# First loads of a fused attention and two-layer kernel: queues, order and warm-up

## The chip, the core and the metric

One NeuronCore of a Trainium2 chip runs the whole kernel. The engines named below are TensorE (PE, with its weight loads PEld), VectorE (DVE), ScalarE (ACT) and SyncE (SP). SP only starts DMAs here; ACT computes and can start DMAs too. An engine works through its own instructions in the order in which they are written, so a DMA that waits on ACT's queue holds back what ACT has to compute behind it. The metric is the device time of one execution in microseconds (us), lower is better.

## What is computed

Retention attention without a softmax, over 4 batches, 8 heads, 576 positions and head dimension 64, and then two feed-forward layers over the 2304 tokens, all in float32:

```python
scores = scale * np.matmul(q, k.transpose(0, 1, 3, 2))
Dmat = np.where(rel >= 0, gamma[:, None, None] ** rel[None, :, :], 0.0)
x = np.matmul(scores * Dmat[None], v)          # -> 2304 x 512
h = x @ w_in;  x = (np.maximum(h, 0) + np.log1p(np.exp(-np.abs(h)))) @ w_out
r = np.maximum(x @ w2_in, 0);  out = (r * r) @ w2_out
```

The first layer goes 512 to 2048 to 512, the second likewise.

## The kernel before

The sequences are cut into chunks of 64 positions, and two chunks together are one loaded "chunk c" of 128 tokens, 18 in all. The decay factors are worked into k, v and a table, so attention is a chain over chunks: scores, a mask, a running state and the output.

The first four chunks (`last = 4`) make the first tile of 512 tokens and are written out by hand at the head of the kernel, under `tc.manual_schedule()`, so each engine runs its instructions in exactly the written order. This head is the place of the change. For each chunk c of 0 to 3:

- `early_qk(c)` (L968) loads q and k with head dimension on the partitions, heads 0 to 3 to partitions 0 to 63 (LO) and heads 4 to 7 to 64 to 127 (HI): two DMAs of 256 KB, in rows of 1024 bytes. `early_kv(c)` (L977) loads k and v with tokens on the partitions: one DMA of 512 KB over 128 partitions. Both issue from the sync queue.
- `early_scores(c)` (L992, PE) multiplies k and q of the chunk, `early_mask(c)` (L1013, DVE) applies the causal mask, `early_v(c)` (L1001, DVE) scales v, `early_states(c)` (L1024, PE, kept by ACT at L1030) updates the state, `early_carried(c)` and `early_o(c)` (L1040, L1048, PE) make the output, and `early_x(c)` (L1062, DVE, then a rounding copy on ACT, L1067) multiplies it with a table of factors.
- That table is made in the kernel: `rows_in` holds two rows of factors, `spread_rows()` (L1121) spreads them over partitions by matmuls, ACT copies them out (L1125, L1126), and `scalar_xw` (L1131, ACT) and `make_xw` (L949, DVE) multiply them up. `make_xw(1, 1)` stands on DVE between `early_v(0)` and `early_mask(1)`; `early_x(0)` needs it.

Ahead of the first scores, `keep_warm(n)` runs n dummy matmuls of 512 columns on PE (each counts twice in the trace, as float32 goes through PE in two passes). `cst` holds the mask, the factors of v and two rounding constants (two DMAs of 34.5 KB); the first weights `wi_raw` follow the chunks on the sync queue. Splitting a weight into two reduced-precision parts takes ACT L152, L153, then DVE L157, L160, then ACT L188 and DVE L189. The first real layer matmuls are L1096 (`early_g1`) and the steady loop is L515 and L549.

The framework gives DMAs their completion semaphores in rotation, eight of them shared by both queues: a DMA waits, on the engine that issues it, until the DMA that held its semaphore before has landed. No line of the kernel writes these waits.

Of the kernel before, what the change touches and what calls it, by code (L numbers as in the profile page):

```python
# [16 lines left out]
P = 128  # L17
D = 64
CN = 64
# [21 lines left out]
C_ONE, C_UP, C_VW, C_MASK, C_XW = 0, 1, 2, 74, 138  # L41
# [4 lines left out]
def kernel(  # L46
# [26 lines left out]
    nc = tc.nc  # L73
# [33 lines left out]
    cst = const.tile([P, C_ALL], F32, name="cst")  # L107
# [172 lines left out]
    def pump_load(upto):  # L280
        while n_load[0] < min(upto, len(loads)):
            load_w(*loads[n_load[0]])
            n_load[0] += 1
# [68 lines left out]
    LO, HI = slice(0, P // 2), slice(P // 2, P)  # L352
# [5 lines left out]
    def load_chunk(c):  # L358
        if c < NPR:
            new_chunk(c)  # L360
            for i, src in ((0, qk_t), (2, kv)):
                nc.sync.dma_start(
                    out=chunk[c][:, i:i + 2],
                    in_=src[2 * c:2 * c + 2].rearrange("s p i h c -> (s p) i h c"),
                )
# [563 lines left out]
    def keep_warm(count, n=512):  # L929

        for _ in range(count):
            nc.tensor.matmul(
                cold[:, :n], lhsT=warm[:, :P], rhs=warm[:, :n], start=True, stop=True
            )
# [11 lines left out]
    def make_xw(m, n):  # L946


        nc.vector.scalar_tensor_tensor(  # L949
            out=later[:, m - 1:m - 1 + n],  # L950
            in0=cst[:, x_first].rearrange("p (a b) -> p a b", a=KD).unsqueeze(1)
            .to_broadcast([P, n, KD, CN]),
            scalar=1.0,
            in1=times[:, m - 1:m - 1 + n].unsqueeze(3).to_broadcast([P, n, KD, CN]),
            op0=ALU.mult, op1=ALU.mult,
        )
# [4 lines left out]
    qks, kvs, mixed, kept_s, pbs, pos, xs_of, kept_of = {}, {}, {}, {}, {}, {}, {}, []  # L961
    causal = first_pool.tile([P, P], F32, tag="causal", name="causal", bufs=1)

    def early_tiles(c):
        qks[c] = first_pool.tile([P, 2, 2, HH, CN], F32, tag=f"qk{c}", name="qk", bufs=1)
        kvs[c] = first_pool.tile([P, 2, H, CN], F32, tag=f"kv{c}", name="kv", bufs=1)

    def early_qk(c):  # L968
        for g, half in enumerate((LO, HI)):
            nc.sync.dma_start(  # L970
                out=qks[c][half].rearrange("p i s h c -> p i s (h c)"),
                in_=qk_t[2 * c:2 * c + 2].rearrange("s p i h c -> p i s (h c)")[
                    ..., g * HH * CN:(g + 1) * HH * CN
                ],
            )

    def early_kv(c):  # L977
        nc.sync.dma_start(
            out=kvs[c], in_=kv[2 * c:2 * c + 2].rearrange("s p i h c -> (s p) i h c")
        )  # L980

    def early_scores(c):
        if c % 2:
            pb = pbs[c] = [ps_h.tile([P, 512], F32, tag=f"h{g}", name="pb") for g in range(2)]
        else:
            pb = ps_head.tile([P, 2, 512], F32, tag="pb", name="pb", bufs=1)
            pbs[c] = [pb]
            pb = [pb[:, g] for g in range(2)]
        for hh in range(HH):
            for s, to in enumerate((LO, HI)):  # L990
                for g, rows in enumerate((LO, HI)):
                    nc.tensor.matmul(  # L992
                        pb[g][to, hh * P:(hh + 1) * P],
                        lhsT=qks[c][rows, 1, s, hh, :], rhs=qks[c][rows, 0, :, hh, :],
                        start=True, stop=True, skip_group_check=True,
                    )

    def early_v(c):
        t = kvs[c][:, 1]
        w = vw[:, 2 * c * H:(2 * c + 1) * H]  # L1000
        nc.vector.tensor_tensor(  # L1001
            out=t, in0=t, in1=w.unsqueeze(2).to_broadcast([P, H, D]), op=ALU.mult
        )

    def early_mask(c):
        mixed[c] = first_pool.tile([P, H, P], F32, tag="mixed", name="mixed")
        for g, pb in enumerate(pbs[c]):
            n = H // len(pbs[c])
            if len(pbs[c]) == 1:
                pb = pb.rearrange("p g (h n) -> p (g h) n", n=P)  # L1010
            else:
                pb = pb.rearrange("p (h n) -> p h n", n=P)
            nc.vector.tensor_tensor(  # L1013
                out=mixed[c][:, g * n:(g + 1) * n], in0=pb,
                in1=causal.unsqueeze(1).to_broadcast([P, n, P]), op=ALU.mult,
            )
# [53 lines left out]
    def early_keep(c):  # L1070
        nc.sync.dma_start(out=x0d[:, :, c * P:(c + 1) * P], in_=kept_of[c])
# [40 lines left out]
    def spread_rows():  # L1112
        rows = ps_head.tile([P, 2, 512], F32, tag="po", name="rows", bufs=1)
        to = [
            rows[:, 0, at:at + n * b].rearrange("p (a b) -> p a b", a=n)
            for at, n, b in ((0, KD, CN), (256, SCN - 1, KD))
        ]
        for half in (LO, HI):
            one = slice(half.start, half.start + 1)
            for r, of in zip(to, (row[0][:, 0], row[0][:, 1:, :, 0])):  # L1120
                nc.tensor.matmul(  # L1121
                    r[half], lhsT=ones[one], rhs=of[one],
                    start=r is to[0], stop=True, skip_group_check=True,
                )
        nc.scalar.copy(cst[:, x_first].rearrange("p (a b) -> p a b", a=KD), to[0])  # L1125
        nc.scalar.mul(times, to[1], float(D) ** 0.5)  # L1126

    def scalar_xw(m, n):
        for m in range(m, m + n):
            for a in range(KD):  # L1130
                nc.scalar.activation(  # L1131
                    out=later[:, m - 1, a], in_=cst[:, C_XW + a * CN:C_XW + (a + 1) * CN],
                    func=AF.Copy, scale=times[:, m - 1, a:a + 1],
                )

    with tc.manual_schedule():
        rows_in = xs.tile([P, SCN * KD * CN], F32, tag="xr", name="rows_in")
        for c in range(last):
            early_tiles(c)
        early_qk(0)  # L1140
        for half in (LO, HI):
            nc.scalar.dma_start(out=cst[half, :C_XW], in_=consts[CN:P, :C_XW])
        early_kv(0)
        early_qk(1)
        early_kv(1)
        for r in (0, CN):
            nc.scalar.dma_start(out=rows_in[r:r + 1], in_=consts[r:r + 1, C_XW:])
        nc.scalar.preload_act_table_set("softplus")
        for c in range(2, last):
            early_qk(c)  # L1150
            early_kv(c)
        pump_load(3)
        load_chunk(last)
        nc.vector.memset(causal[LO, CN:], 1.0)
        nc.vector.memset(causal[HI, :CN], 0.0)

        for half, to, of, n in ((LO, 0, 0, SCN), (HI, 0, 1, SCN - 1), (HI, SCN - 1, 0, 1)):
            nc.vector.tensor_copy(
                vw[half, to * H:(to + n) * H], cst[half, C_VW + of * H:C_VW + (of + n) * H]
            )  # L1160
        for s, half in enumerate((LO, HI)):
            nc.vector.tensor_copy(
                causal[half, s * CN:(s + 1) * CN], cst[half, C_MASK:C_MASK + CN]
            )
        keep_warm(6)
        early_scores(0)
        row.append(rows_in.rearrange("p (m a b) -> p m a b", a=KD, b=CN))
        spread_rows()
        keep_warm(1)
        scalar_xw(4, 2)  # L1170
        early_mask(0)
        early_v(0)
        make_xw(1, 1)
        early_scores(1)
        early_states(0)
        early_mask(1)
        early_v(1)
        early_carried(0)
        early_o(0)
        early_x(0)  # L1180
        early_scores(2)
        early_states(1)
        scalar_xw(6, 1)
        early_carried(1)
        early_o(1)
        make_xw(2, 2)
        early_mask(2)
        early_v(2)
        early_x(1)
        scalar_xw(7, 2)  # L1190
        early_scores(3)
        early_states(2)
        early_carried(2)
        early_o(2)
        early_low(0)
        early_mask(3)
        early_v(3)
        begin_words()
        early_keep(0)
        early_x(2)  # L1200
        next(begun[0])
        early_low(1)
        early_keep(1)
        early_states(3)
        early_carried(3)
        early_o(3)
        next(begun[0])
        begun.clear()
        begin_words()
        early_g1(0)  # L1210
        early_x(3)
        next_state(3, 1)
        begin_words()
        early_low(2)
        early_low(3)
        early_keep(2)
        for made in begun:
            next(made)
        early_keep(3)
# [231 lines left out]
```

## Time and profile before

| | us |
|---|---|
| three timed runs | 825.25, 827.16, 827.66 |
| their median | 827.16 |
| profiled execution, its time | 823.74 |
| profiled execution, span of the trace | 822.0 |
| PE busy in the span | 810.8 (99%) |
| DVE busy in the span | 607.2 (74%) |
| ACT busy in the span | 378.9 (46%) |

The profiled execution is a single one, 3.4 us below the median of the timed runs. Busy shares cover stages with different limits; the change touches only the first 20 us or so, so what matters there is read from the chain of waits, the timeline and the stretches of that part. In a timeline row the first number is the start in us, the second the length, and a bracket at the end says how long the engine idled before and what released it.

### The profile page before, as it was taken

To read this page: it belongs to the slowest core of one execution; us is meant where nothing else is said; L and a number is where in the kernel's file an instruction comes from. 1 tells how busy PE (TensorE), PEld (TensorE's weight loads), DVE (VectorE), ACT (ScalarE), POOL (GpSimd) and SP (SyncE) were. 2 spreads that over 40 slices of the span, in tenths; PEclk is the share of its full clock that TensorE was granted. 3 is DMA by queue.
4 is the path that set the end of the run, shared out by engine and by line. 5 is a ranking of instruction groups with operands and counts; after the bars stand their busy time and mean duration, and the time that the engine had idled before them with its cause. 6 is when DMAs were issued, how large, how long until landed. Compare 5 with 4: busy or idle time off the path is not lost.

```text
span 822.0 us, 16243 instructions
## 1 busy us (share of the span) xinstructions
PE 810.8 (99%) x5957; PEld 721.6 (88%) x5957; DVE 607.2 (74%) x1160; ACT 378.9 (46%) x739; POOL 0.2 (0%) x4
## 2 busy tenths in 40 slices
PE   8898999999999999999999999999999999999998
PEld 5777999988888888888999999988999988999887
DVE  4998766646565664646796498998798997787876
ACT  3787666535344543545665221454211554111553
POOL 0000000000000000000000000000000000000000
PEclk9999999999999999999999999999999999999999
DMA  9967554466666655656979387898978889888885
GB/s 238 310 219 239 180 180 124 134 207 215 209 229 213 194 172 188 197 181 211 300 251 300 94 251 248 271 297 285 299 249 254 250 271 282 282 249 249 251 274 170
DMA packets 122802, 189.37 MB, mean 230 GB/s; under 512 B 10466, under 2 KB 68450, under 8 KB 122722
## 3 DMA queue, kind: packets, MB, share of 16 engines
q1 hardware_dynamic: 122560, 188.26, 72.1%
q8 instruction: 47, 0.77, 0.4%
q14 instruction: 31, 0.25, 0.1%
q10 hardware_dynamic: 164, 0.09, 0.1%
HBM read 147.41 MB, written 40.89 MB: 229 GB/s over the span
## 4 chain that ended last, share of the span: by engine, by line
PE 95%; DMA 3%; DVE 1%; ACT 0%; SPq 0%; issue 0%; DVEq 0%; ACTq 0%
PE acc L549 24%; PE ph L515 24%; PE py L685 9%; PE py L758 9%; PE px L685 6%; PE pz L758 6%; PE px L758 6%; PE pz L685 6%; PE po L439 2%; DMA qk<-in_qk_t_dram 1%; PE pb L391 1%; PE st L416 1%; DMA kv<-in_kv_dram 1%; DMA ring<-in_qk_t_dram 1%; SPq L970 0%
## 5 line engine op out<-in xcount | busy, mean ns | idle before, releaser
L515 PE MATMUL ph<-xh,wi 128*128 128x512 f32 (+1 forms) x632 | 144.4, 370 | 1.3 <-DVE wi L189 0.8
L515 PEld LDWEIGHTS ph<-xh,wi 128*128 128x128 f32 x632 | 115.9, 189 | 17.0 <-DVE wi L189 1.2
L549 PE MATMUL acc<-gh,woh 128*128 128x512 f32 (+1 forms) x320 | 120.5, 377 | 0.0
L549 PE MATMUL acc<-gh,wol 128*128 128x512 f32 (+1 forms) x320 | 117.8, 368 | 0.0
L549 PE MATMUL acc<-gl,woh 128*128 128x512 f32 (+1 forms) x320 | 117.8, 368 | 0.0
L534 DVE TENSOR_TENSOR gl<-e,gh 128x512 fp32r<-128x512 f32 (+1 forms) x80 | 51.0, 637 | 71.1 <-ACT gh L533 70.3
L526 ACT ACTIVATE e<-ph 128x512 f32<-128x512 f32 (+1 forms) x80 | 44.3, 554 | 126.4 <-PE ph L515 126.2
L685 PE MATMUL py<-t,sring 128*128 128x384 f32 x432 | 88.3, 338 | 0.0
L515 PE MATMUL ph<-xl,wi 128*128 128x512 f32 (+1 forms) x316 | 78.2, 369 | 0.0
L685 PEld LDWEIGHTS py<-t,sring 128*128 128x128 f32 x432 | 74.8, 188 | 2.5 <-DVE uring L889 0.5
L549 PEld LDWEIGHTS acc<-gh,woh 128*128 128x128 f32 x320 | 60.0, 188 | 8.6
L549 PEld LDWEIGHTS acc<-gh,wol 128*128 128x128 f32 x320 | 60.1, 188 | 7.7
L549 PEld LDWEIGHTS acc<-gl,woh 128*128 128x128 f32 x320 | 60.1, 188 | 6.9
L515 PEld LDWEIGHTS ph<-xl,wi 128*128 128x128 f32 x316 | 58.5, 190 | 7.6
L738 ACT CAST gh<-g 128x384 fp32r<-128x384 f32 x84 | 43.2, 515 | 46.2 <-PE px L758 16.1
L738 ACT CAST gring<-g 128x384 fp32r<-128x384 f32 x84 | 43.2, 515 | 39.9 <-PE py L758 16.2
L685 PE MATMUL pz<-t,sring 128*128 128x384 f32 x288 | 58.3, 334 | 0.0
L685 PE MATMUL px<-t,sring 128*128 128x384 f32 x288 | 58.0, 335 | 0.0
L401 DVE TENSOR_TENSOR ring<-pb,cst 64x256 f32<-64x256 f32 x56 | 23.6, 422 | 44.1 <-PE pb L391 27.2
L706 DVE TENSOR_TENSOR g<-g 128x384 f32<-128x384 f32 x96 | 52.6, 554 | 1.5
L706 DVE TENSOR_TENSOR gring<-g,gring 128x384 fp32r<-128x384 f32 x84 | 46.2, 553 | 9.5 <-ACT gring L738 8.3
L706 DVE TENSOR_TENSOR gl<-g,gh 128x384 fp32r<-128x384 f32 x84 | 46.5, 554 | 8.8 <-ACT gh L738 7.7
(123 smaller groups left out, 1403.2 us busy)
## 6 DMA issues: line engine op xcount, KB each, us to landing
sring<-s2d SPq DMA_DIRECT2D x168, 256.0 KB, 3.1
sring<-o2d SPq DMA_DIRECT2D x168, 256.0 KB, 3.2
wi_raw<-in_moe_w_in_dram SPq DMA_DIRECT2D x32, 512.0 KB, 4.9
wo_raw<-in_moe_w_out_dram SPq DMA_DIRECT2D x32, 512.0 KB, 4.1
s2d<-ct SPq DMA_DIRECT2D x48, 256.0 KB, 2.8
o2d<-ct SPq DMA_DIRECT2D x48, 256.0 KB, 3.4
ring<-in_qk_t_dram SPq DMA_DIRECT2D x14, 512.0 KB, 4.1
ring<-in_kv_dram SPq DMA_DIRECT2D x14, 512.0 KB, 6.3
```

The source lines that it names most:

```text
L391: nc.tensor.matmul(pb[to, h, :], lhsT=kk[:, hh, :], rhs=qp[:, hh, :], start=True, stop=True, skip_group_check=True,)
L401: nc.vector.tensor_tensor(out=chunk[c][rows, 1, i * HH:(i + 1) * HH], in0=pb[of], in1=mask[of], op=ALU.mult)
L416: nc.tensor.matmul(st[to, h, :], lhsT=kk[:, hh, :], rhs=sv[:, hh, :], start=m == h == 0, stop=True, skip_group_check=True,)
L439: nc.tensor.matmul(po[(LO, HI)[hh % 2], hh // 2, :], lhsT=before[rows, hh, :] if carried else sv[:, hh, :], rhs=qp[:, hh, :] if carried el ...
L515: nc.tensor.matmul(ph[:, :n], lhsT=a, rhs=x, start=(j == 0), stop=(j == len(todo) - 1))
L526: nc.scalar.activation(out=g, in_=hps.pop(key)[:, :n], func=AF.Softplus)
L534: nc.vector.tensor_tensor(out=l[:, :n], in0=g, in1=h[:, :n], op=ALU.subtract)
L549: nc.tensor.matmul(acc[j][:, :n], lhsT=a, rhs=x, start=(begin and m == 0), stop=(end and m == 2))
L685: nc.tensor.matmul(ps, lhsT=a, rhs=x, start=(first and m == 0), stop=(m == len(todo) - 1), skip_group_check=True,)
L706: nc.vector.tensor_tensor(out=out, in0=a, in1=b, op=ALU.subtract)
L738: nc.scalar.copy(h, src)
L758: nc.tensor.matmul(blocks[m][:, :cols], lhsT=a[:, c], rhs=x, start=(first and p == n == 0), stop=(p == NP - 1 and n == len(todo) - 1), ski ...
```

## The change

The two constant DMAs go first, one on each queue. The halves of q and k of each of the first chunks are issued on two queues instead of one: the lower partitions by sync, the upper by scalar. k and v become two DMAs of 256 KB, k by sync and v by scalar. The two rows of factors are issued directly behind the first q and k. `keep_warm(6)` becomes `keep_warm(4)`. The loop over chunks 2 and 3 uses the same functions, so their upper halves and v also move to the scalar queue.

```diff
     def early_qk(c):
-        for g, half in enumerate((LO, HI)):
-            nc.sync.dma_start(
+        for g, (half, queue) in enumerate(((LO, nc.sync), (HI, nc.scalar))):
+            queue.dma_start(
                 out=qks[c][half].rearrange("p i s h c -> p i s (h c)"),
...
     def early_kv(c):
-        nc.sync.dma_start(
-            out=kvs[c], in_=kv[2 * c:2 * c + 2].rearrange("s p i h c -> (s p) i h c")
-        )
+        for i, queue in enumerate((nc.sync, nc.scalar)):
+            queue.dma_start(
+                out=kvs[c][:, i],
+                in_=kv[2 * c:2 * c + 2, :, i].rearrange("s p h c -> (s p) h c"),
+            )
...
         for c in range(last):
             early_tiles(c)
+        for half, queue in ((LO, nc.scalar), (HI, nc.sync)):
+            queue.dma_start(out=cst[half, :C_XW], in_=consts[CN:P, :C_XW])
         early_qk(0)
-        for half in (LO, HI):
-            nc.scalar.dma_start(out=cst[half, :C_XW], in_=consts[CN:P, :C_XW])
+        for r in (0, CN):
+            nc.scalar.dma_start(out=rows_in[r:r + 1], in_=consts[r:r + 1, C_XW:])
         early_kv(0)
         early_qk(1)
         early_kv(1)
-        for r in (0, CN):
-            nc.scalar.dma_start(out=rows_in[r:r + 1], in_=consts[r:r + 1, C_XW:])
         nc.scalar.preload_act_table_set("softplus")
         for c in range(2, last):
             early_qk(c)
...
-        keep_warm(6)
+        keep_warm(4)
         early_scores(0)
```

## Rows read from the trace of the kernel before

**Rows 1.** The page's chain that ended last, shares of the span by engine.

```profile
PE 95%; DMA 3%; DVE 1%; ACT 0%; SPq 0%; issue 0%; DVEq 0%; ACTq 0%
```

**Rows 2.** Chain of waits, 0 to 40 us: start us, length us, what.

```profile
2.29 6.64 DMA kv<-in_kv_dram
...
9.58 9.78 DMA qk<-in_qk_t_dram
...
19.40 1.10 PE pb L992 x30
...
24.20 0.71 DVE ct L160
...
31.64 4.38 PE ph L515 x11
```

**Rows 3.** Windows: PE, PEld, DVE, ACT, POOL busy, granted clock, DMA share, GB/s.

```profile
5.70:6.70 1.00, 1.00 (x4) 0.41 (x3) 0.00 (x0) 0.00 (x0) 0.00 (x0) 1.00 0.93 334
7.10:8.50 1.40, 1.40 (x8) 0.40 (x6) 0.00 (x0) 0.00 (x0) 0.00 (x0) 1.00 1.13 216
...
11.10:12.50 1.40, 1.40 (x39) 1.06 (x40) 0.79 (x3) 1.40 (x7) 0.00 (x0) 1.00 1.11 209
...
19.50:22.50 3.00, 3.00 (x78) 2.58 (x79) 2.00 (x4) 2.75 (x11) 0.00 (x0) 1.00 1.09 351
...
30.80:32.20 1.40, 0.56 (x2) 0.48 (x3) 1.31 (x3) 1.15 (x2) 0.00 (x0) 0.99 0.94 290
32.20:35.60 3.40, 3.40 (x9) 2.67 (x8) 3.00 (x6) 1.62 (x4) 0.00 (x0) 0.50 0.94 320
```

**Rows 4.** Timeline, 5 to 9 us: TensorE, the last dummy matmuls and first scores.

```profile
5.81 0.19 PEld L932 LDWEIGHTS cold<-warm 128*128 128x128 f32 x1 [0.24 <-issue]
6.24 0.19 PEld L932 LDWEIGHTS cold<-warm 128*128 128x128 f32 x1 [0.24 <-issue]
...
8.48 1.10 PE L992 MATMUL pb<-qk 64*64 64x128 f32 x32
```

**Rows 5.** Timeline of the two DMA-issuing queues, SP and ACT.

```profile
0.73 1.20 ACTq L1142 DMA_DIRECT2D cst<-in_consts_dram  x2
...
4.70 0.34 SPq L978 DMA_DIRECT2D kv<-in_kv_dram  x1
...
8.94 1.26 SPq L970 DMA_DIRECT2D qk<-in_qk_t_dram  x2
```

**Rows 6.** DMA issues at 0.73, 1.54, 2.29 and 4.70 us: last number us to landing.

```profile
qk<-in_qk_t_dram SPq DMA_DIRECT2D x1, 256.0 KB, 4.0
...
qk<-in_qk_t_dram SPq DMA_DIRECT2D x1, 256.0 KB, 4.5
...
kv<-in_kv_dram SPq DMA_DIRECT2D x1, 512.0 KB, 6.6
...
kv<-in_kv_dram SPq DMA_DIRECT2D x1, 512.0 KB, 8.3
```

**Rows 7.** Timeline, 10 to 23 us: steps of ACT and DVE that set the pace.

```profile
10.33 0.37 ACT L1125 COPY cst<-rows 128x256 f32<-128x256 f32 x1 [6.02 <-PE rows L1121]
...
11.39 0.42 DVE L949 SCALAR_TENSOR_TENSOR cst<-cst,times 128x256 f32<-128x256 f32 x1
...
12.42 1.29 DVE L1013 TENSOR_TENSOR mixed<-pb,causal 128x512 f32<-128x512 f32 x2 [0.61 <-PE pb L992]
...
16.10 1.23 DVE L1013 TENSOR_TENSOR mixed<-pb,causal 128x1024 f32<-128x1024 f32 x1 [0.59 <-PE pb L992]
...
18.33 0.69 DVE L1062 TENSOR_TENSOR x<-po,cst 128x512 f32<-128x512 f32 x1 [0.40 <-PE po L1048]
...
20.54 1.29 DVE L1013 TENSOR_TENSOR mixed<-pb,causal 128x512 f32<-128x512 f32 x2 [0.92 <-PE pb L992]
...
22.10 0.69 ACT L152 ACTIVATE wi_raw<-wi_raw 128x512 f32<-128x512 f32 x1 [0.25 <-DMA wi_raw<-in_moe_w_in_dram]
...
22.78 0.69 DVE L1062 TENSOR_TENSOR x<-po,cst 128x512 f32<-128x512 f32 x1 [0.36 <-PE po L1048]
```

## The prediction, made before the change was run

> **What bounds the kernel now.** I read the page's chain first: 95% of the span is TensorE's own work [rows 1], so only a small part can be given back by anything else, and that part lies at the head. The chain of waits of the first 40 us shows it: a kv load from 2.29 us, then a q and k load from 9.58 that lands at 19.36, chunk 3's scores at 19.40, and from 22.8 on an unbroken run of VectorE and ScalarE steps that split weights (L160 at 24.20) until the steady matmuls start at 31.64 [rows 2]. So the head is a load-bound stretch (to 19.4), then an elementwise-bound one (to 31.6). Behind it TensorE is full, and a head that is shorter by d makes the kernel shorter by d and by no more.
>
> Next, stretches inside the load-bound part. The DMA engines are busy all the time, but not at one rate: 334 GB/s while a kv load (128 partitions) moves, 216 and 209 GB/s while a half of q and k (64 partitions) moves, 351 GB/s with the 128-partition weights [rows 3]. So a chunk's q and k, 512 KB (524 KB in thousands), takes 524/212 = 2.47 us, where at 351 it would take 1.49. That is 0.98 us a chunk and 3.9 us over four: the most that the split over two queues can win in the loads.
>
> Last, the timeline of the elementwise engines. VectorE waits, between 12 and 23 us, 0.61 + 0.59 + 0.40 + 0.92 + 0.36 = 2.9 us for TensorE, which at those places mostly waits for loads, and ScalarE's first weight step at 22.10 waits 0.25 us for its load [rows 7]. These waits are what an earlier load can remove.
>
> **The change, part by part.**
>
> *Warm-up.* Two dummy matmuls less are four passes less, at 6.24 - 5.81 = 0.43 us each: 1.72 us. TensorE would reach the first scores at 8.48 - 1.72 = 6.76 [rows 4]. The second half of chunk 0's q and k landed at 1.54 + 4.5 = 6.04 [rows 6]. Now a constant DMA of 1.20/2 = 0.60 us of issue [rows 5] stands in front of it, but the halves start together. Bounds: 6.04 + 0.60 = 6.64 if they gain nothing, about 5.3 at the full rate (0.98 less for the pair, and upper half issued at 1.3 instead of 1.54). Either way before 6.76, so the first scores come 1.7 us earlier. The passes that went slowly are the first ones, which stay.
>
> *Loads.* Split over two queues, the halves can move at the same time and together cover 128 partitions. Ends: 0 and 0.98 us a chunk. The halves won't be in step (next part), so I take two thirds, 0.65, nearer to the 128-partition row because the two halves in flight together cover what a kv load covers. Against it, 0.5 us later for the constants in front. The kv load in two parts of 256 KB moves the same bytes to the same 128 partitions; the weights' rows are as short as q's and k's and run at 351 [rows 3], so I cost that at nothing. Chunk 1's kv landed at 4.70 + 8.3 = 13.0 [rows 6]; now 13.0 + 0.5 - 1.3 = 12.2 (11.5 to 13.5). Chunk 3's q and k: 19.36 + 0.5 - 2.6 = 17.3 (15.9 to 19.9). First weight: 22.1 + 0.5 - 2.6 = 20.0 (18.7 to 22.6).
>
> The Trainium skill speaks against this step. Its page "SBUF — State Buffer" (section "Can I just issue two DMAs to hit both halves?") states that two concurrent DMAs, one on each half of the partitions, were measured only 6% faster than one. By that the pair would take 2.33 instead of 2.47 us, four chunks would win 0.6, and the constants would take that back. The rows here show only that 64 partitions are slow and 128 fast; none has two halves in flight from two queues, so I keep it as a rival with its own chance.
>
> *ScalarE's queue.* This is the price. ScalarE issued four DMAs, and its first computation (the copy of the factor rows at 10.33) waited for TensorE alone, after 6.02 us of idling [rows 7]. Now it issues eleven, the last of them v of chunk 3, all ahead of that copy; the load of the function table, too, lies among them and ends before it. A DMA is not issued until the eighth before it, over both queues, has landed: the kv issue at 4.70 came as the first q and k landed (0.73 + 4.0), the issue at 8.94 as chunk 0's kv landed (2.29 + 6.6) [rows 5, 6], each eight earlier when the scalar queue's are counted in. Counting the new order with the queues taking turns, v of chunk 3 is the 21st and waits for the 13th, v of chunk 1: 12.2. With 0.34 us of issue [rows 5] the copy starts at about 12.6, 2.3 us later than before. If sync runs ahead by two, it waits for a part of chunk 2's kv instead, some 1.5 to 2 us later; if the loads are at the full rate, 11.5.
>
> Who waits for the copy: the factors (0.5 us on ScalarE), then make_xw(1, 1) on VectorE, at 13.1 instead of 11.39, and behind it in VectorE's order everything else. So the 1.7 us won at the first scores are lost here.
>
> *The sum along VectorE.* make_xw +1.75. mask(1) before waited 0.61 for scores, which are there now: +1.15, at 13.6. v(1), x(0) the same. mask(2) before waited 0.59, chunk 2's scores are there: +0.55. x(1) before waited 0.40; output 1 ends at about 17.8 and x(1) comes at 18.5: +0.15. mask(3) before waited 0.92 for the scores of 19.40; these run now at 17.8 to 18.9: mask(3) at 19.75, -0.8. x(2) before waited 0.36: 21.65, -1.1. ScalarE, though, makes the rounding copy of x(1) at +0.15, then its eight table steps, and reaches the weight at 22.10 + 0.15 - 0.25 = 22.0; L152 and L153 end at 23.4, and L160 comes at about 23.5 instead of 24.20 [rows 2, 7]. That is 0.7 us earlier. From there to 31.64 the steps of both engines follow each other and nothing from memory is late, so the gain goes through: steady matmuls at 30.9.
>
> Against the profiled execution: 823.74 - 0.7 = 823.0. The timed runs have a median of 827.16, 3.4 us above the profiled one; the same 0.7 taken from it gives 826.5. A measurement of this kernel can tell about 0.3%, 2.5 us, from no change.
>
> **The rivals.**
>
> *The loads reach the full rate and ScalarE is released before it matters.* For it: 334 and 351 GB/s on 128 partitions. If the copy came by about 9.5, make_xw would follow v(0) at 9.9; mask(1) is then held by its scores to 10.9 (-1.5), mask(2) to 14.2 (-1.9), x(1) comes at 16.0 (-2.3), and the weight step at 19.7 (-2.4). That gives 824.8. Against it: the copy stands behind the last v, whose issue hangs on a landing that the loads' rate alone keeps from coming before about 11.
>
> *The halves don't help and ScalarE is held: slower.* If two half loads share the engines without gain, chunk 1's v lands at 13.2 to 13.5, the copy comes at about 13.8, make_xw at 14.3 (+2.9). The four removed waits of VectorE no longer cover this: mask(2) +1.7, the copy of x(1) on ScalarE +1.3, the weight step +1.1, L160 (then set by ScalarE) some +0.9 to +1.4. It decides at a copy later than about 13.3, where the sum gives zero (0.7 of gain at 12.6, a slope of about one). Price 1.0 us: 828.2. The same comes about at a faster load if sync runs ahead and the last v waits for chunk 2. The skill's rule named above leads here.
>
> *The clock.* From 32.2 to 35.6 the granted clock was 0.50, the lower level of 1.2 GHz, just after a stretch in which TensorE was busy 0.56 of 1.40 us [rows 3]; 3.4 us at half speed cost 1.7 us. A head that is shifted may miss this fall: 826.5 - 1.7 = 824.8; or, with fewer dummy matmuls and the wait for the factors in the middle, get a second one: 828.2.
>
> *That it doesn't do what it says:* the later issues depend on landings, so the two halves may go out of step and run one after the other; this ends in the slower case.
>
> **How the numbers follow.** Forecast (0.7 gained) 0.42; full rate with early release 0.22; slower by the held ScalarE 0.23; clock 0.13. The likeliest gives 826.5, with 825.3 to 827.7 for its own range (the three runs spread by 2.4 us). For 8 in 10 I go down past the full-rate case to 823.5 and up past the slower one to 828.7. Faster by over 0.3% needs 824.7 or less: half of the full-rate and of the clock case and a little of the forecast, 0.23. Slower by over 0.3% needs 829.6: a part of the slower case, 0.07. The rest, 0.70, is within.
>
> **What would show it.** First scores at 6.8 us instead of 8.48. In the stretch 5 to 12 us, GB/s above 300 if the halves run together, 215 if not. ScalarE's copy L1125 near 12.6, and VectorE's L949 near 13.1 with a wait on ScalarE before it: if it comes at 10 the first rival holds, after 13.3 the second. Chunk 3's scores without a wait for a load, near 17.8. L152 at 22.0, L160 at 23.5, first run of L515 at 30.9. The prediction is wrong if the steady matmuls start before 29.5 or after 32.5, or if the time moves by more than the head does.

## The result, and the profile after

The changed kernel is slower: 835.41 us against 826.95, medians of six runs each (832.96 to 839.43 and 825.25 to 828.41), a ratio of 1.0105 with a 95% interval of 1.0075 to 1.0135. The forecast was 826.5 with a range up to 828.7. The profiled execution took 832.96 us with a span of 830.7, where before had 823.74 and 822.0. (In the table of experiments, the 827.36 of the kernel before beside e7 and e10 includes one slow run of 2061.03 us, which their ratios leave out.)

The page of the kernel after: busy time of each engine, and the shares of the chain that ended last.

```profile
PE 813.2 (98%) x5953; PEld 723.3 (87%) x5953; DVE 607.9 (73%) x1160; ACT 378.6 (46%) x739; POOL 0.2 (0%) x4
...
PE 86%; DMA 6%; DVE 4%; ACT 2%; issue 1%; SPq 0%; DVEq 0%; ACTq 0%
```

TensorE's share of the chain fell from 95% [rows 1] to 86%; what took its place is DMA, VectorE and ScalarE, so a piece without TensorE has become longer. The chain of waits of the kernel after, first 40 us (start, length, what), shows which.

```profile
2.98 5.72 DMA qk<-in_qk_t_dram
...
8.72 7.33 DMA qk<-in_qk_t_dram
...
16.07 10.45 DMA qk<-in_qk_t_dram
...
26.56 1.10 PE pb L994 x30
...
31.35 0.70 DVE ct L160
```

Chunk 3's scores ran at 26.56 instead of 19.40, and the first VectorE step on the weights, L160, at 31.35 instead of 24.20 [rows 2]: 7.15 us later. (Lines after the changed functions are two higher than before.) From 2.98 to 26.52 this chain is three loads, one behind the other. The lower half of chunk 1's q and k, issued by sync at 2.98, landed at 2.98 + 5.72 = 8.70; at 8.72 scalar issued the upper half of the same chunk, which landed at 16.05; at 16.07 it issued the upper half of chunk 3, which landed at 26.52. All three carry the same completion semaphore in the trace, so each was issued only when the one before it had landed. The timeline of the kernel after shows what the two queues did meanwhile; queue SP first, then queue ACT.

```profile
1.39 0.85 SPq L970 DMA_DIRECT2D qk<-in_qk_t_dram  x1
2.29 0.64 SPq L979 DMA_DIRECT2D kv<-in_kv_dram  x1
2.98 0.60 SPq L970 DMA_DIRECT2D qk<-in_qk_t_dram  x1
...
6.61 0.60 SPq L970 DMA_DIRECT2D qk<-in_qk_t_dram  x1
7.77 0.33 SPq L979 DMA_DIRECT2D kv<-in_kv_dram  x1
9.87 1.90 SPq L132 DMA_DIRECT2D wi_raw<-in_moe_w_in_dram  x3
```

```profile
1.35 0.65 ACTq L970 DMA_DIRECT2D qk<-in_qk_t_dram  x1
2.04 1.39 ACTq L1146 DMA_DIRECT2D rows_in<-in_consts_dram  x2
6.10 0.37 ACTq L979 DMA_DIRECT2D kv<-in_kv_dram  x1
8.72 0.61 ACTq L970 DMA_DIRECT2D qk<-in_qk_t_dram  x1
...
18.15 0.34 ACTq L979 DMA_DIRECT2D kv<-in_kv_dram  x1
```

By 7.77 sync had issued all eight of its loads, of all four chunks, and from 9.87 on it issued weights; scalar had by 7.77 issued two of its eight, the upper half of chunk 0 and v of chunk 0, and brought the last one out at 18.15. So chunks 1 to 3 had their lower halves and k early, which are of little use alone (two of the 32 matmuls of chunk 1's scores ran at 10.67, the others waited), and their upper halves and v late, with weights in front of them. What the engines made of it, same view:

```profile
7.88 1.10 PE L994 MATMUL pb<-qk 64*64 64x128 f32 x32
...
12.59 0.69 DVE L1003 TENSOR_TENSOR kv<-kv,vw 128x512 f32<-128x512 f32 x1 [2.32 <-DMA kv<-in_kv_dram]
16.09 1.98 PE L994 MATMUL pb<-qk 64*64 64x128 f32 x30 [5.00 <-DMA qk<-in_qk_t_dram]
18.54 0.37 ACT L1127 COPY cst<-rows 128x256 f32<-128x256 f32 x1 [6.14 <-DMA kv<-in_kv_dram]
19.04 0.43 DVE L949 SCALAR_TENSOR_TENSOR cst<-cst,times 128x256 f32<-128x256 f32 x1 [5.75 <-ACT times L1128]
19.38 1.28 DVE L1015 TENSOR_TENSOR mixed<-pb,causal 128x512 f32<-128x512 f32 x2
```

Chunk 1's mask came at 19.38 instead of 12.42 [rows 7], +6.96. Its scores ended at 16.09 + 1.98 = 18.07, so 5.65 of this is late data (0.9 of it the lower clock, see below); the remaining 1.3 is ScalarE's copy, held behind the last DMA of its queue until 18.54. But this 1.3 is not in the time at the end, since at chunk 3 TensorE, and VectorE behind it, waited for a load once more. Same view, later:

```profile
26.56 1.10 PE L994 MATMUL pb<-qk 64*64 64x128 f32 x30 [1.51 <-DMA qk<-in_qk_t_dram]
...
27.70 1.29 DVE L1015 TENSOR_TENSOR mixed<-pb,causal 128x512 f32<-128x512 f32 x2 [1.67 <-PE pb L994]
```

VectorE was free 1.67 us before the mask of chunk 3 could run, more than the 1.3 that the copy had cost it. An earlier copy alone would only have made this wait longer.

Windows of the kernel after: columns as in [rows 3].

```profile
2.80:5.50 2.70, 2.70 (x4) 1.01 (x3) 0.84 (x5) 0.00 (x0) 0.00 (x0) 1.00 0.99 230
5.00:12.00 7.00, 6.10 (x49) 2.85 (x47) 1.22 (x1) 0.89 (x1) 0.00 (x0) 1.00 1.09 265
14.00:20.70 6.70, 4.61 (x62) 4.08 (x62) 1.66 (x4) 2.13 (x9) 0.00 (x0) 0.50 1.10 300
```

Three readings. While chunk 0's two halves moved, 2.8 to 5.5 us, the rate was 230 GB/s, near the 216 and 209 of halves from one queue and far from the 334 to 351 over 128 partitions [rows 3]. From 5 to 12 us the DMA engines moved as much as before (265 GB/s; before, 261): the bytes came no slower, only in the wrong order. And after TensorE's 5.00 us of idling the granted clock was 0.50, the 1.2 GHz level, so that the scores of chunk 1 took 1.98 us instead of 1.10.

### The profile page after: what moved, and what is told of

It is laid out like the page before. It is cut to its first block, busy times and chain, and to the rows that moved or that the text cites. A ratio compares the mean times of both kernels' runs of the same rounds, so it can differ in the third digit from the quotient of the medians.

```text
span 830.7 us, 16239 instructions
## 1 busy us (share of the span) xinstructions
PE 813.2 (98%) x5953; PEld 723.3 (87%) x5953; DVE 607.9 (73%) x1160; ACT 378.6 (46%) x739; POOL 0.2 (0%) x4
## 3 DMA queue, kind: packets, MB, share of 16 engines
q1 hardware_dynamic: 121552, 186.20, 71.4%
## 4 chain that ended last, share of the span: by engine, by line
PE 86%; DMA 6%; DVE 4%; ACT 2%; issue 1%; SPq 0%; DVEq 0%; ACTq 0%
PE acc L549 21%; PE ph L515 19%; PE py L685 9%; PE py L758 9%; PE px L685 6%; PE pz L758 6%; PE px L758 6%; PE pz L685 6%; DMA qk<-in_qk_t_dram 3%; PE po L439 2%; DMA wo_raw<-in_moe_w_out_dram 2%; PE st L416 1%; PE pb L391 1%; DVE ct L160 1%; DMA ring<-x2d 1%
## 5 line engine op out<-in xcount | busy, mean ns | idle before, releaser
L515 PE MATMUL ph<-xh,wi 128*128 128x512 f32 (+1 forms) x632 | 143.3, 368 | 2.3 <-ACT ring L427 1.0
L515 PEld LDWEIGHTS ph<-xh,wi 128*128 128x128 f32 x632 | 115.4, 188 | 18.0 <-ACT ring L427 1.4
L515 PE MATMUL ph<-xl,wi 128*128 128x512 f32 (+1 forms) x316 | 77.6, 367 | 0.0
L515 PEld LDWEIGHTS ph<-xl,wi 128*128 128x128 f32 x316 | 57.9, 188 | 7.4
```

The source lines that it names most:

```text
L515: nc.tensor.matmul(ph[:, :n], lhsT=a, rhs=x, start=(j == 0), stop=(j == len(todo) - 1))
```

## The experiments

The expectations of the first runs weigh three theories: that scalar's loads are issued late because sync runs ahead in the shared semaphores, with ScalarE's own work held behind them (A); that two queues share the DMA engines without gain and all loads land later (B); and that fewer dummy matmuls and the clock cost the time (C). From e9 on the two parts of A are set against each other, late data and the held ScalarE. The expectations of e8 and e7 take a wait for the first factor row as the cause of the late data; the chains of waits below show other waits in their place.

Each kernel ran with the kernel before on the same chip; times are medians in us, the ratio has its 95% interval. The next to last column is the start of the first real layer matmul (L515, or L516 where a line was added) in the profiled execution (one for each kernel), less the 30.29 of before; the last one is what the ratio amounts to at 827 us.

| kernel | time | before | ratio | head, us | ratio in us |
|---|---|---|---|---|---|
| after | 835.41 | 826.95 | 1.0105 (1.0075 to 1.0135) | +7.14 | +8.7 |
| e1_order_only | 826.32 | 825.97 | 1.0008 (0.9990 to 1.0025) | +0.65 | +0.7 |
| e2_qk_split | 829.67 | 825.97 | 1.0053 (1.0030 to 1.0075) | +3.34 | +4.4 |
| e3_kv_split | 826.98 | 825.97 | 1.0024 (1.0006 to 1.0042) | +1.53 | +2.0 |
| e4_chunk0_split | 829.65 | 825.97 | 1.0050 (1.0033 to 1.0068) | +3.26 | +4.1 |
| e8_chunk0_rows_on_sync | 827.22 | 826.35 | 1.0007 (0.9987 to 1.0027) | +0.85 | +0.6 |
| e9_chunks01_split | 833.30 | 826.35 | 1.0079 (1.0054 to 1.0103) | +8.13 | +6.5 |
| e7_all_rows_on_sync | 833.03 | 827.36 | 1.0070 (1.0044 to 1.0095) | +5.87 | +5.8 |
| e11_all_rows_on_pool | 829.41 | 827.11 | 1.0030 (1.0014 to 1.0046) | +2.16 | +2.5 |
| e12_two_rows_on_pool | 828.33 | 827.11 | 1.0007 (0.9992 to 1.0021) | +1.66 | +0.6 |
| e5_one_load | 825.87 | 826.35 | 0.9987 (0.9972 to 1.0001) | -0.14 | -1.1 |
| e6_one_load_warm4 | 823.65 | 826.35 | 0.9964 (0.9946 to 0.9982) | -2.66 | -3.0 |
| e10_one_load_warm2 | 825.70 | 827.36 | 0.9986 (0.9971 to 1.0001) | -2.95 | -1.2 |

The two last columns agree within 1.8 us in every row: to that accuracy, what the head loses or wins is what the kernel loses or wins.

### One part of the change alone: e1, e2, e3

All three keep the change's order of constants and factor rows and its four dummy matmuls. e1 issues all of q, k and v by sync, as before; e2 splits only q and k over the queues; e3 splits only k and v. The edits to the changed kernel, e1 (both), e2 (the second) and e3 (the first):

```diff
-        for g, (half, queue) in enumerate(((LO, nc.sync), (HI, nc.scalar))):
+        for g, (half, queue) in enumerate(((LO, nc.sync), (HI, nc.sync))):
...
-        for i, queue in enumerate((nc.sync, nc.scalar)):
-            queue.dma_start(
-                out=kvs[c][:, i],
-                in_=kv[2 * c:2 * c + 2, :, i].rearrange("s p h c -> (s p) h c"),
-            )
+        nc.sync.dma_start(
+            out=kvs[c], in_=kv[2 * c:2 * c + 2].rearrange("s p i h c -> (s p) i h c")
+        )
```

> The changed order of the constants and the factor rows and the 4 dummy matmuls, with q, k and v of all chunks back on the sync queue. Theory A (the scalar queue's loads are issued late, because the sync queue runs ahead and takes the eight shared DMA semaphores, and ScalarE's own work stands behind them): nothing of that is left, so ScalarE's factor copy comes at 9 to 10.5 us and the time is that of before, 825 to 828. Theory B (two queues share the engines without gain, all loads land later): also the time of before. Theory C (fewer dummy matmuls, a clock that rises later and falls again, cost the time): 830 or more, the granted clock falls in the first 25 us.

> As the changed kernel, but k and v in one load on the sync queue; q and k stay split over two queues. Theory A: upper halves of chunks 1 to 3 are issued late by ScalarE, the factor copy comes at 13 to 17 us: 829 to 834. Theory B: the same loss for the halves, but it is in the landing, not in the issue: the pair of halves issued together takes 2.4 us or more from the first to the second landing, all loads 1 us later, 827 to 829. Theory C: as the changed kernel, 834 or more.

> As the changed kernel, but both halves of q and k on the sync queue; k and v stay split. Theory A: ScalarE issues four v loads, the last behind an early load of the eighth before; factor copy at 12 to 17 us, v of chunk 1 late: 828 to 833. Theory B: nothing is slower than before in the loads (128 partitions each): 826 to 828. Theory C: 834 or more.

The order and the shorter warm-up alone do nothing (e1, 1.0008), which leaves theory C no room. Splitting q and k alone costs about half of the loss (e2, 1.0053), though ScalarE is not held there: its copy came at 10.57. So the theory that the held copy makes the loss has no room in e2. Splitting k and v alone, which puts the v of all four chunks on ScalarE's queue, cost little (e3, 1.0024); v of chunk 0 went out at 3.10, and its copy came at 10.53. Theory A had asked for 828 to 833 here, and missed with 826.98. Timeline of e2:

```profile
6.52 0.62 ACTq L970 DMA_DIRECT2D qk<-in_qk_t_dram  x1
...
14.71 1.98 PE L992 MATMUL pb<-qk 64*64 64x128 f32 x30 [4.06 <-DMA qk<-in_qk_t_dram]
```

The upper half of chunk 1 went out at 6.52, where sync had issued the lower one at 2.96, and the scores waited for it until 14.71. By the chain of waits it was released as the lower half of chunk 0, on sync's queue, landed at 6.50.

### One chunk split, and the wait behind it: e4, e8, e9

e4 splits only chunk 0 and loads chunks 1 to 3 by sync as before; e8 is e4 with the two factor rows issued by sync instead of scalar; e9 splits chunks 0 and 1.

```diff
-        for g, (half, queue) in enumerate(((LO, nc.sync), (HI, nc.scalar))):
+        for g, (half, queue) in enumerate(((LO, nc.sync), (HI, nc.scalar if c == 0 else nc.sync))):
...
     def early_kv(c):
+        if c:
+            nc.sync.dma_start(
+                out=kvs[c], in_=kv[2 * c:2 * c + 2].rearrange("s p i h c -> (s p) i h c")
+            )
+            return
```

In e9 the two conditions are `c < 2` and `c > 1`. e8 adds:

```diff
         for r in (0, CN):
-            nc.scalar.dma_start(out=rows_in[r:r + 1], in_=consts[r:r + 1, C_XW:])
+            nc.sync.dma_start(out=rows_in[r:r + 1], in_=consts[r:r + 1, C_XW:])
```

> As the changed kernel, but only chunk 0 is split over the two queues; chunks 1 to 3 are loaded as before. Theory A: ScalarE has issued its last load by about 7 us, the factor copy waits for TensorE alone (about 9.5): the time of before, 825 to 828. Theory B: chunk 0 lands 0.5 us later, the rest as before: 826 to 828. Theory C: 834 or more. If v of chunk 0 still lands after 11 us, the order in which the engines serve the two queues matters even for one chunk, and the time is 1 to 2 us above before.

> As e4 (chunk 0 alone split over two queues), but the two rows of factors are issued by the sync queue in the same place, so that v of chunk 0 on the scalar queue is issued directly behind its q and k half and waits for no semaphore. Theory A, in the form that e4 left (v of chunk 0 was issued at 6.8 us, after the landing of the first factor row, and the engines serve transfers in the order of issue over both queues, so it stood behind all that sync had issued): v is issued near 2.1 us, VectorE scales it before 11 us, time 825.5 to 827. Rival (a 2048-byte-row load or the scalar queue itself is served slowly): v still lands 6 us or more after its issue, VectorE scales it after 13 us, time 828.5 or more.

> As the changed kernel, but chunks 2 and 3 are loaded as before, by sync alone; ScalarE's last issue is v of chunk 1 and its factor copy is released some 6 us earlier than in the changed kernel. If the late data of chunk 1's upper half set the time: scores of chunk 1 still complete near 16 us, time 831 to 834. If ScalarE's hold behind the loads of chunks 2 and 3 set it: most of the loss of the changed kernel goes, 827 to 829.

e4 missed its expectation, and was the run that turned the theory: a late v was named there as a sign, but priced at 1 to 2 us. With one chunk split, ScalarE's copy came at 9.26, earlier than before, and yet the kernel lost 0.5%. The timeline of e4, and its chain of waits:

```profile
6.80 0.38 ACTq L984 DMA_DIRECT2D kv<-in_kv_dram  x1
...
15.23 0.69 DVE L1008 TENSOR_TENSOR kv<-kv,vw 128x512 f32<-128x512 f32 x1 [5.43 <-DMA kv<-in_kv_dram]
```

```profile
1.38 5.40 DMA qk<-in_qk_t_dram
...
6.80 8.40 DMA kv<-in_kv_dram
```

v of chunk 0, the third thing that anybody needs, was issued at 6.80 and landed 8.4 us later, behind what sync had issued for later chunks. Why at 6.80: by the chain it was released when the lower half of chunk 0, issued by sync at 1.38, landed at 1.38 + 5.40 = 6.78, and the two carry the same semaphore in the trace. It did not wait for the first factor row, as e8's expectation has it; the semaphore of that row went to the upper half of chunk 2. The eight semaphores are handed out when the program is built, and the trace shows them in another order than that in which the DMAs were issued, so that the eighth before by the text is not the one waited for. e8 moves the two rows alone, and with them the rotation. The timeline of e8, and the DMA issue (its last number is us to landing):

```profile
2.04 0.62 ACTq L984 DMA_DIRECT2D kv<-in_kv_dram  x1
...
9.89 0.68 DVE L1008 TENSOR_TENSOR kv<-kv,vw 128x512 f32<-128x512 f32 x1
```

```profile
kv<-in_kv_dram ACTq DMA_DIRECT2D x1, 256.0 KB, 5.5
```

v now waits for nothing, goes out at 2.04 and lands 5.5 us later, VectorE scales it at 9.89, and the loss is gone (1.0007; its 827.22 is just over the 825.5 to 827 expected). The edit also makes sync issue later (k of chunk 0 at 3.14 instead of 2.10), so the 0.4% between e4 and e8 is for the order of the two queues as a whole; that the factor rows themselves held anybody here is not shown. e9 looks from the other side: with two chunks split, ScalarE has four loads less than in the changed kernel. Timeline of e9:

```profile
14.00 0.37 ACT L1132 COPY cst<-rows 128x256 f32<-128x256 f32 x1
...
18.91 1.98 PE L999 MATMUL pb<-qk 64*64 64x128 f32 x30 [7.65 <-DMA qk<-in_qk_t_dram]
```

The copy came 4.5 us earlier than in the changed kernel, and most of the loss stayed (1.0079): chunk 1's scores waited for its upper half until 18.91. A held copy is not what the loss hangs on.

### The queues kept in step: e7, e11, e12

e7 takes e8's edit, the factor rows by sync, into the changed kernel with all four chunks split. e11 gives the rows to GpSimd's queue, which has nothing else to do. e12 is e11 with only chunks 0 and 1 split, so that ScalarE's queue holds four loads less.

```diff
         for r in (0, CN):
-            nc.scalar.dma_start(out=rows_in[r:r + 1], in_=consts[r:r + 1, C_XW:])
+            nc.gpsimd.dma_start(out=rows_in[r:r + 1], in_=consts[r:r + 1, C_XW:])
```

> The changed kernel with the two factor rows issued by sync instead of scalar, all else as changed. If only the one wait of scalar behind the slow factor row was at fault: 826 to 828, as e8. If the fault is that one queue runs ahead in the shared semaphores whichever it is, the roles change: scalar issues chunk 0 and 1 at once, sync's k of chunk 0 waits for a factor row and stands behind scalar's loads; ScalarE is released before 11 us but k or the lower half of chunk 1 lands after 13 us: 829 to 833.

> The changed kernel with the two factor rows issued by the idle GpSimd queue: now sync and scalar have the same loads in the same order ahead of them, so neither runs ahead in the shared semaphores. Theory A (the loss of the changed kernel is the run-ahead, and the two halves in step neither win nor lose): v of chunk 0 issued at 2.1 us, chunk 1's upper half near 2.7, scores of chunk 1 without a 5 us gap; what is left is ScalarE's hold behind its last load, whose wait ends near 12 to 13 us: factor copy at 12.5 to 13.5, 826 to 829. Rival (the split itself, with two queues in the engines, costs the loss): scores of chunk 1 complete after 15 us, 831 or more. If the halves in step do move faster: GB/s above 300 between 3 and 12 us and 823 to 825.

> As e11, but chunks 2 and 3 are loaded by sync alone, so ScalarE issues its last load (v of chunk 1) near 4 us and its factor copy waits for TensorE alone, at 9 to 10.5 us. Beside e11 this is the price of the hold: if the hold costs what the prediction gave (about 1 us of VectorE's chain for each us of copy later than 12), e12 is 1 to 2 us faster than e11, 825 to 827. If VectorE has that slack anyway, both are the same.

In e7 the roles are exchanged: now scalar runs ahead, and sync issued k of chunk 0 only at 7.94. By the chain of waits it was released by v of chunk 0, which scalar had issued at 2.04 and which landed at 7.92; the factor rows are not in the chain here either. Timeline of e7:

```profile
8.34 0.60 SPq L970 DMA_DIRECT2D qk<-in_qk_t_dram  x1
10.14 0.37 ACT L1127 COPY cst<-rows 128x256 f32<-128x256 f32 x1 [4.87 <-DMA qk<-in_qk_t_dram]
...
16.38 1.98 PE L994 MATMUL pb<-qk 64*64 64x128 f32 x32 [6.19 <-DMA qk<-in_qk_t_dram]
```

It is the lower half of chunk 1 that is late now (issued at 8.34), the scores start at 16.38, within 0.3 us of the changed kernel, and the loss is 1.0070, although ScalarE's copy is free at 10.14. Which queue runs ahead doesn't matter; that one does, does. In e11 the rows have semaphores of their own, and neither queue runs ahead for chunks 0 and 1, whose loads go out in pairs at most 0.3 us apart (for chunks 2 and 3 scalar is 1.7 to 3.4 us behind). Timeline and a window of e11:

```profile
2.05 0.62 ACTq L979 DMA_DIRECT2D kv<-in_kv_dram  x1
12.60 1.98 PE L994 MATMUL pb<-qk 64*64 64x128 f32 x32 [2.52 <-DMA qk<-in_qk_t_dram]
15.39 0.37 ACT L1127 COPY cst<-rows 128x256 f32<-128x256 f32 x1 [10.10 <-DMA qk<-in_qk_t_dram]
```

```profile
3.00:9.00 6.00, 6.00 (x48) 2.79 (x46) 1.29 (x6) 1.28 (x1) 0.00 (x0) 1.00 1.03 223
```

v of chunk 0 goes out at 2.05, chunk 1's scores at 12.60 instead of 16.09, and most of the loss is gone (1.0030). This is the change with both queues in step for two chunks, and it still wins nothing: the rate is 223 GB/s from 3 to 9 us, kv loads included, where the kernel before had 256. Its copy is held to 15.39, which is the price that the prediction had in mind. e12 shortens ScalarE's queue, its copy comes at 9.08 and its first layer matmul 0.5 us earlier (1.0007). But the chain of waits of e11 does not pass through the copy:

```profile
2.98 9.58 DMA qk<-in_qk_t_dram
...
12.58 8.95 DMA qk<-in_qk_t_dram
...
21.57 1.10 PE pb L994 x30
```

It runs from the lower half of chunk 1 to the upper half of chunk 3, issued by scalar as the other landed, and to chunk 3's scores. e12 loads chunk 3 by sync again, so the step from e11 to e12, 0.5 us by the profiles and 1.9 by the ratios, with intervals that just overlap, holds both the freed copy and the earlier load. What the hold costs by itself was not measured.

Taken step by step, by the ratios: from the changed kernel to e11, 1.0105 - 1.0030, is 6.2 us for the queue that runs ahead (the copy, too, came 3.1 us earlier); from e11 to e12 1.9 us for chunks 2 and 3 back on sync; 0.6 us are left, no different from zero. By the start of the first layer matmul the three are 5.0, 0.5 and 1.7 us.

### One load over 128 partitions: e5, e6, e10

The reverse test of the load rate: the kernel before, with q and k of the first four chunks from an extra input that holds the same numbers in the order of the partitions, so that one DMA of 512 KB in rows of 4096 bytes fills all 128 partitions. The new order is made outside the kernel, and its cost is not in the time. e6 is e5 with `keep_warm(4)`, e10 with `keep_warm(2)`.

```diff
     def early_qk(c):
-        for g, half in enumerate((LO, HI)):
-            nc.sync.dma_start(
-                out=qks[c][half].rearrange("p i s h c -> p i s (h c)"),
...
+        nc.sync.dma_start(out=qks[c], in_=qk_f[c])
```

> The kernel before, with q and k of the first four chunks taken from an input that is laid out so that one load fills all 128 partitions (4096 bytes in each); all else, the 6 dummy matmuls too, as before. If a load to 64 partitions is slow because of the 64 partitions (the step of the prediction that priced a half at 2.47 us a pair and a full load at 1.49): chunk 3's q and k land at 15.5 us instead of 19.4, VectorE's waits of 12 to 23 us go, steady matmuls 2 to 2.5 us earlier, time 823.5 to 824.5. If it is slow for another reason (short rows, start of the kernel): landing as before and 826.

> As e5, with 4 dummy matmuls in place of 6. If the loads no longer bind, the first scores at 6.8 to 8 us pass 0.5 to 1.7 us on: 822 to 824. If something else of the elementwise engines binds: as e5. If a clock that rises later costs it: above e5.

> The one-load version with 2 dummy matmuls. Its first q and k landed at 4.4 us in e6, while the dummies held TensorE to 7.7: without two more of them the first scores come at 5 to 6.5 us if the clock rises as late as there, and the elementwise chain 1 to 2 us earlier: 821.5 to 823.5. If the clock then stays at its lower level through the first chunks, or the factor rows (second one landed at 8.0 in e6) hold TensorE: 823.5 to 825.

The window 5 to 12 us of e5, and of e6:

```profile
5.00:12.00 7.00, 7.00 (x51) 3.27 (x49) 2.13 (x6) 0.76 (x4) 0.00 (x0) 1.00 1.03 399
```

```profile
5.00:12.00 7.00, 7.00 (x96) 3.90 (x95) 3.21 (x8) 2.45 (x10) 0.00 (x0) 1.00 1.03 401
```

In this stretch 399 and 401 GB/s move, where before had 261. The load differs in two things, 128 partitions and longer rows; that the weights, with 1024 bytes in a row on 128 partitions, moved at 351 [rows 3] speaks for the partitions as the greater part. In e5 the six dummy matmuls hide the gain: the first scores came at 9.35, behind them, the head won 0.14 us, and e5 missed its 823.5 to 824.5. With four (timeline of e6):

```profile
7.66 1.10 PE L987 MATMUL pb<-qk 64*64 64x128 f32 x32
...
27.63 0.50 PE L516 MATMUL ph<-xh,wi 128*128 128x512 f32 x1 [0.40 <-ACT wi L189]
```

the head is 2.66 us shorter and the kernel 0.36% faster (0.9946 to 0.9982): e6 is faster than both kernels. Two dummies (e10, 825.70, outside the 821.5 to 825 expected) gave no more: its first scores started at 5.15, but ran at the lower clock (1.99 us instead of 1.10), and its head is only 0.29 us shorter than that of e6. Its 0.9986 reaches to 1.0001, and whether it is slower than e6 or only scattered stays open.

## Why the prediction was wrong

**What bounds the kernel: right.** A head longer by d makes the kernel longer by d: the table shows it over thirteen kernels, within 1.8 us. In the changed kernel the delay is 7.15 us at L160, and 7.12 still some 40 us later (the same step of L160 at 71.85 instead of 64.73). In the profiled execution another 1.2 us came behind the head (the L160 at 90.35 stood at 82.06 before), past a clock fall to 0.50, which stood at 32.2 to 35.6 before and in the profile after at 78.8 to 82.2, where TensorE is full:

```profile
78.80:82.20 3.40, 3.40 (x10) 2.66 (x9) 3.22 (x7) 2.61 (x5) 0.00 (x0) 0.50 0.77 193
```

Whether such falls make the same 1.3 us between the medians (8.5 us, less the 7.14 of the head) is not shown: e1 and e8 had one, too, in their profiles (from 72.3 and from 71.4 us) and lost nothing by their ratios.

**Warm-up: right in kind, a third in size.** The passes left out are worth 0.43 us each only at the full clock. The first scores came at 7.88 instead of 8.48: 0.6 won, where 1.72 were forecast. Passes ran 0.85 us apart until the granted clock rose at 7.13, while in the profile before it rose near 4.9. "The passes that went slowly are the first ones, which stay" was the sentence that failed.

**Loads: wrong.** 0.65 us a chunk was taken, and nothing was won. Chunk 0's halves, issued 0.04 us apart, landed 3.9 and 5.2 us later, one behind the other, at 230 GB/s. e11, with two chunks in step, moved 223. The rule of the Trainium skill that the prediction kept as a rival ("SBUF — State Buffer", section "Can I just issue two DMAs to hit both halves?": only 6% over a single one) agrees with 230 against 209 and 216, and e5 shows its other half: one transfer over 128 partitions reaches 399. The nearest row had been taken wrongly: a kv load covers 128 partitions in one DMA, and that, not what is in flight together, was what made it fast. That k and v in two parts cost nothing in rate was right: e3 moved 252 GB/s from 3 to 12 us, and so did e1, which loads them whole.

**ScalarE's queue: the step that failed.** "Counting the new order with the queues taking turns" put the last v at 12.2 and the copy at 12.6; they came at 18.15 and 18.54. That the last v waits for v of chunk 1 was right (it is the 20th for the 12th in the order given, not the 21st for the 13th; nothing hangs on that): the two carry the same semaphore, and v of chunk 1, issued at 10.72, landed at 18.13. What failed is "the queues taking turns", which let v of chunk 1 land at 12.2. The rotation is fixed in the program, in another order, and in it four of scalar's loads waited for a load of sync's that was still under way, as the upper half of chunk 1 did at 8.72 for its own lower half; v of chunk 0 waited, to 6.10, for the first factor row. The bound for it, "if sync runs ahead by two", was too near: sync ran ahead by all the rest of its queue, and into the weights.

**What was left out altogether** is larger than what was mis-sized. The prediction priced a late issue by what ScalarE computes behind it. It never asked who waits for the load itself. A load that was issued late stood behind what the other queue had issued before, so the upper halves and v came late for TensorE and VectorE, whatever ScalarE did. That is 5.65 of the 6.96 us at chunk 1's mask, and all of the chain from 2.98 to chunk 3's scores at 26.56; by the step to e11 it is some 5 (by the head) to 6 (by the ratios) of the 8.7 us in the end. The rival "it doesn't do what it says" named the halves out of step, and the slower rival had its sign; both were priced with 1.0 us because only the held copy was in the sum. That copy stands on the chain of waits of neither the changed kernel nor e11.

**Clock rival: a part.** A second fall came in the middle of the head, as it says (0.50 from 14.0 to 20.7), and cost the scores of chunk 1 0.9 us; that is within the 5.65 above. The 1.7 us that it priced the fall at 32.2 with were not there to win: from the first layer matmul at 30.29 to L160 at 64.73 the profile before took 34.44 us with that fall, and the changed kernel, from 37.43 to 71.85, 34.42 without one.

What stays open is the share of the clock: where its rise and its later fall stand differs from kernel to kernel, and each was seen in one execution of each.

## What to carry to other kernels

Splitting a tile's load by partitions over two queues brought no bandwidth here; one DMA over all 128 partitions did, which needs the data in memory laid out for it. Before loads are moved to a second queue, find out which DMA each of them waits for (here a load of the other queue more often than one of its own), and ask of the late ones first who needs the data and only then what they hold up on their engine. Moving two small transfers to another queue changed which load waits for which, and with it the time by 0.4%. After any gain in the loads, look at what is next in front of the first use; here it was the warm-up, and only both together (e6) were faster; e5 has the one load alone, and e1 the shorter warm-up with the change's order.

## What the runs showed of the hardware that was not expected

- In the changed kernel and e4, until about 17 us, the loads of both queues landed about in the order of their issue. In e4 v of chunk 0 was alone on the scalar queue when it was issued at 6.80. It landed at 15.2, after the kv of chunk 1, which sync had issued at 4.29 (landed at 12.4), and before the kv of chunk 2, issued at 7.68 (17.3). An estimate from the windows of e4: by 6.80 sync and scalar had issued 2.36 MB of loads; from 2.8 on 218 GB/s had moved 0.87 MB of them; the 1.49 MB left take 5.7 us at the 260 GB/s of 6.8 to 15.2, the load itself 1.0: 6.7 of the 8.4 us. With half of the rate for the scalar queue it would have been 2.0, and 1.4 from issue to first bytes (1.35 to 2.8 at the start): 3.4. Later in the changed kernel it is otherwise: chunk 2's upper half, issued by scalar at 13.59, landed after 7.7 us, at 21.3, ahead of a load of weights that sync had issued at 11.40:

```profile
wi_raw<-in_moe_w_in_dram SPq DMA_DIRECT2D x1, 512.0 KB, 13.2
```

  What makes the difference stays open. The Trainium skill ("DMA: Bandwidth & Descriptors", section "Issuing engines are not separate DMA queues") says that DMAs of several queues run on the same engines and interleave. That two queues moved no more than one agrees (230 GB/s); an interleaving that helps the later load shows only in the second of these two cases.
- One DMA over 128 partitions in rows of 4096 bytes moved 399 and 401 GB/s, more than the 351 of the weights [rows 3].
- The granted clock rose between 4.65 and 7.63 us after the start in these fourteen kernels, and fell once for about 3.4 us to the lower level between 68 and 82 us in eleven of them, not in before, e3 and e9. In the changed kernel, where it fell at 78.8, TensorE had been busy for 1.57 of the 3.8 us from 75 on.
